# Attention, gated MLP and MoE on one core: the first three tiles' loads at once, the last routing, the sorting and the overflow list at other places

## The chip, the cores and the metric

The kernel runs on one core of a Trainium2 chip. The metric is the device time of one execution in microseconds. Three runs of the kernel before gave 929.73, 930.45 and 933.15 us; the median is 930.45.

## What is computed

Three layers follow each other over N = 3072 tokens (4 sequences of 768) of 384 numbers. All data are float32.

```python
# 1. attention with a decaying state: 8 heads of 48, per token t
cur = einsum('bhd,bhe->bhde', u * k[t], v[t])
y[t] = einsum('bhd,bhde->bhe', r[t], state + cur)
state = w[t][..., None] * state + einsum('bhd,bhe->bhde', k[t], v[t])
# 2. RMS norm and gated MLP, 384 -> 1536 -> 384
xn = x / sqrt(mean(x * x) + 1e-06) * rms_g
x = (silu(xn @ w_gate) * (xn @ w_val)) @ w_out
# 3. MoE: 8 experts, one per token, 384 -> 1024 -> 384
e_idx = argmax(x @ moe2_w_gate)
for e in range(8):
    mask = e_idx == e
    out[mask] = softmax_prob[mask, e] * sigmoid(x[mask] @ w_output_gate)[:, e] \
              * (relu(x[mask] @ w1[e]) @ w2[e])
```

The MLP's weights reach the kernel as 64-bit floating-point words, which it turns into float32 itself.

## The kernel before

**Numbers in two halves.** A matmul of float32 is made of three matmuls on a high and a low half (`mm3`, L163 to L167). The high half is written by ScalarE (ACT), the low half (value minus high half) by VectorE (DVE) or GpSimd (POOL), and TensorE (PE) needs both. For the experts' weights that is `split` (L133 to L135), for a relu `relu_split` (L870 to L878), for gathered tokens `transpose_in` (L572 to L583).

**The stretches.** Tokens go in tiles of 128 and the MLP in 8 blocks of 3 tiles. The attention of a tile is a Python generator, `attention` (L338 to L460), that issues a few instructions per step. The first three tiles and the first block of the MLP are the start; from then on each block's MLP runs with the attention of the next block and the routing of the block before between its matmuls, placed by a small table of slots (`Plan`). After the last block comes the second MoE, in units of tokens of one expert.

**The attention of a tile.** `load_tile` (L302 to L315) loads the features w, k and r in a transposed layout, as two pairs of DMAs on SyncE's (SP's) queue: w (96 KB each) and k with r (192 KB each). They land in one of two standing buffers, and tile 2's in a slot of the ring of weight buffers, which is free so early. Such a buffer has rows that no load writes; `pads` (L278 to L284) fills them, for tile 2 on POOL. `load_rk` (L317 to L321) loads r and k by rows (384 KB) into `rk`, of which there is one buffer; the generator of tile i asks for tile i+1's loads once its own data are used. `load_v` loads v (192 KB). Then follow the product r*k*u on POOL (L363, L364), its row sums g on DVE (L380), the output y (DVE, L384 and L424, and PE, L420), a copy of transposed k on ACT (L393) and the state's update.

**The MLP's weights.** 18 pieces are decoded (`decode`, L98 to L132), 12 of the first layer (a piece is one load of 384 KB from each of two matrices) and 6 of the second. A piece takes two DMAs, two passes on ACT (L113 and the high half), two on DVE (L114 and L118), one on POOL and one for the low half. The loads of pieces 0, 1 and 2 are issued ahead of everything (`advance(n, 1)`, L700 to L706); a `decode_step` then issues the loads of piece n+2 and decodes piece n.

**The hand-written start.** `START_SEQ` (L42, run by L711 to L719) is the order of the start: 0, 1 and 2 issue one step of that tile's attention, a negative number issues so many matmuls without use that keep TensorE awake, and 9 is a `decode_step`. All engines run their instructions in this order, so DVE takes up decode step 0 where the first 9 stands.

```python
advance(0, 1)
load_tile(1)
advance(1, 1)
load_v(1)
advance(2, 1)
load_tile(2)
load_v(2)
nc.gpsimd.memset(states, 0.0)
```

**The second MoE.** `route` (L519 and on) finds each token's expert, ranks the tokens within the experts with small matmuls (L552, L555) on the one-hot `oh` from DVE (L544), and scatters the rows to a place per expert in device memory (`scr`). The last block's routing runs inside unit 0 at slots `ROUTE_AT`; a unit has a slot after each group of first-layer matmuls (nine for one f) and of second-layer matmuls. When it is through, the gather of unit 1's tokens is issued on SP and `order()` (L905 to L931) adds up the counts on PE (L909), sorts the experts by size on DVE and hands their numbers to SP, which needs them for the addresses of all later weights and gathers. The units have fixed sizes (`FIRST`, `WINDOWS`: 256, 256, 272, 256, 432, ... tokens); units 0 and 1 are the first expert's, 2 and 3 the largest other one's, numbered from 0 here. Tokens beyond these sizes go on an overflow list, `tabd` in device memory, that `table()` (L933 to L979) makes on DVE in unit 2 at f = 2, and that is read at the end of the kernel. In each unit, f = 0 to 9: first-layer matmuls of f (while f < 8), relu, a share of the next expert's weights (load, split), second-layer matmuls of f - 2; at f = 6 the next unit's tokens are transposed and split.

## Time and profile before

| | |
|---|---|
| three runs | 929.73, 930.45, 933.15 us; median 930.45 |
| the profiled execution | 934.85 us, of which the span of instructions is 933.1 |
| mean granted clock of TensorE | 0.96 |
| PE, weight loads, DVE, ACT, POOL busy | 94%, 91%, 57%, 34%, 24% of the span |
| read and written in device memory | 73.22 MB and 16.73 MB, 96 GB/s over the span |

The profile is of one execution, taken by the hardware profiler. A busy share is an average over the whole span, in which the attention's start, the MLP and the MoE follow each other with limits of their own; so the slices of the span and windows of single stretches are read beside it. An engine's row in a timeline gives behind "[" how long the engine had idled before and, behind "<-", what ended that: `[12.63 <-DMA rk<-in_rkv_dram]` is an idle time of 12.63 us that ended when the load of `rk` landed. PE stands for matmuls, PEld for the weight loads ahead of them, which overlap. The granted clock is a share of TensorE's full rate of 2.4 GHz. "SPq" is SP's queue of DMA issues.

### The profile page before, as it was taken

How to read it: one execution, taken by the hardware profiler on the slowest of the kernel's cores; microseconds unless marked ns; L12 is line 12 of the kernel's file. 1: busy time of each engine (PE TensorE's matmuls, PEld its weight loads, DVE VectorE, ACT ScalarE, POOL GpSimd, SP SyncE). 2: the span in 40 equal slices, each digit the busy share in tenths (PEclk: the TensorE clock that was granted, in tenths of full speed). 3: DMA queues.
4: the chain of work that ended last, by engine and by line, in shares of the span. 5: the costliest groups of instructions: out<-in, count | busy, mean ns of one | idle time of the engine just before them, and what ended most of it. 6: DMA issues, size and time to landing. Idle time of an engine off the chain costs nothing. (4 is left out here: it accounts for less than half of the span.)

```text
span 933.1 us, 14620 instructions
## 1 busy us (share of the span) xinstructions
PE 876.9 (94%) x5543; PEld 846.7 (91%) x5543; DVE 533.7 (57%) x1073; ACT 314.8 (34%) x654; POOL 227.9 (24%) x298
## 2 busy tenths in 40 slices
PE   6568779999999999999999999999899999999995
PEld 4458769999999999999999999999899999999994
DVE  5589785656565376366456465434537565556551
ACT  1254433322322323323222322323334344434430
POOL 6465552212231131132123113010010100122111
PEclk7679899999999999999999999999999999999997
DMA  9564252274131023022122122001143453554510
GB/s 229 129 218 131 90 161 50 83 213 137 46 110 51 9 86 82 13 78 56 47 69 60 52 68 78 1 27 51 52 146 98 151 179 107 159 163 152 174 47 21
DMA packets 65300, 90.40 MB, mean 97 GB/s; under 512 B 6259, under 2 KB 56035, under 8 KB 65229
## 3 DMA queue, kind: packets, MB, share of 16 engines
q1 hardware_dynamic: 60973, 79.67, 29.2%
q0 software_dynamic: 3568, 9.57, 2.8%
q8 instruction: 44, 0.72, 0.3%
q10 hardware_dynamic: 688, 0.22, 0.1%
q14 instruction: 27, 0.22, 0.1%
HBM read 73.22 MB, written 16.73 MB: 96 GB/s over the span
## 5 line engine op out<-in xcount | busy, mean ns | idle before, releaser
L165 PE MATMUL a<-xh,gv 128*128 128x384 f32 x1152 | 324.1, 347 | 0.0
L165 PEld LDWEIGHTS a<-xh,gv 128*128 128x128 f32 x1152 | 213.7, 191 | 2.2
L165 PE MATMUL a<-xl,gv 128*128 128x384 f32 x576 | 195.9, 340 | 0.0
L500 DVE TENSOR_TENSOR sil<-a,sil 128x384 f32<-128x384 f32 x96 | 53.2, 554 | 110.6 <-PE a L165 110.2
L165 PE MATMUL a<-xh,w1s 128*128 128x256 f32 (+7 forms) x432 | 111.9, 325 | 1.4 <-DVE hl L876 1.1
L165 PEld LDWEIGHTS a<-xl,gv 128*128 128x128 f32 x576 | 110.3, 192 | 0.0
L502 ACT ACTIVATE hh<-sil 128x384 fp32r<-128x384 f32 x96 | 50.3, 524 | 162.2 <-DVE sil L500 162.2
L514 PE MATMUL l<-wo,hh 128*128 128x400 f32 x288 | 102.2, 355 | 0.0
L498 ACT ACTIVATE sil<-a 128x384 f32<-128x384 f32 x96 | 47.2, 492 | 156.7 <-PE a L165 151.6
L515 PE MATMUL l<-wo,hh 128*128 128x400 f32 x288 | 99.8, 347 | 0.0
L516 PE MATMUL l<-wo,hl 128*128 128x400 f32 x288 | 99.2, 345 | 0.0
L244 POOL DMA_INDIRECT out_dram<-row,iu x30 | 34.9, 1165 | 208.5 <-DVE row L887 188.7
L876 DVE SCALAR_TENSOR_TENSOR hl<-a,hh 128x256 fp32r<-128x256 f32 (+7 forms) x80 | 40.7, 510 | 74.3 <-ACT hh L875 74.3
L165 PEld LDWEIGHTS a<-xh,w1s 128*128 128x128 f32 x432 | 76.7, 188 | 2.8 <-DVE hl L876 1.6
L505 DVE TENSOR_TENSOR hl<-sil,hh 128x384 fp32r<-128x384 f32 x96 | 56.2, 585 | 34.9 <-ACT hh L502 34.9
L875 ACT ACTIVATE hh<-a 128x256 fp32r<-128x256 f32 (+7 forms) x80 | 36.5, 456 | 101.9 <-PE a L165 100.2
L165 PE MATMUL a<-xl,w1s 128*128 128x256 f32 (+7 forms) x216 | 69.7, 323 | 0.1
L384 POOL TENSOR_TENSOR y<-vt,g 128x384 f32<-128x384 f32 x23 | 22.0, 958 | 169.2 <-issue 62.6
L165 PE MATMUL l<-rows,hh 128*128 128x384 f32 (+3 forms) x240 | 63.0, 344 | 0.0
L420 PE MATMUL m<-vt,am 128*128 128x48 f32 x368 | 55.1, 278 | 4.5 <-DVE am L407 4.5
L420 PEld LDWEIGHTS m<-vt,am 128*128 128x128 f32 x368 | 51.2, 204 | 5.5 <-DVE am L407 5.4
L514 PEld LDWEIGHTS l<-wo,hh 128*128 128x128 f32 x288 | 54.9, 190 | 0.1
(216 smaller groups left out, 1510.8 us busy)
## 6 DMA issues: line engine op xcount, KB each, us to landing
raw<-in_moe_w_dram SPq DMA_DIRECT2D x64, 384.0 KB, 3.3
rk<-in_rkv_dram SPq DMA_DIRECT2D x24, 384.0 KB, 4.2
set<-in_feat_dram SPq DMA_DIRECT2D x46, 192.0 KB, 3.9
scr<-zrow SPq DMA_DIRECT2D x8, 788.0 KB, 7.6
set<-in_feat_dram SPq DMA_DIRECT2D x46, 96.0 KB, 3.0
vt<-in_rkv_dram SPq DMA_DIRECT2D x23, 192.0 KB, 2.5
raw<-in_moe_w_gate_dram SPq DMA_DIRECT2D x8, 384.0 KB, 4.0
raw<-in_moe_w_val_dram SPq DMA_DIRECT2D x8, 384.0 KB, 3.9
```

Source lines behind the costliest of these rows:

```text
L165: nc.tensor.matmul(o, a, b, start=start and i == 0, stop=stop and i == 2, skip_group_check=True)
L244: ins = nc.gpsimd.indirect_dma_start(out=dst, out_offset=bass.IndirectOffsetOnAxis(ap=idx, axis=0), in_=rows, in_offset=None, bounds_check ...
L420: nc.tensor.matmul(yp[:, 2 * p + q], am[q][:, p], vv[:, 2 * p + q], start=not ch, stop=True, skip_group_check=True,)
L498: nc.scalar.activation(out=sil, in_=o, func=AF.Silu)
L500: nc.vector.tensor_tensor(out=sil, in0=pg[1], in1=sil, op=ALU.mult)
L502: nc.scalar.activation(out=hh, in_=sil, func=AF.Copy)
L505: nc.vector.tensor_tensor(out=hl, in0=sil, in1=hh.bitcast(F32), op=ALU.subtract)
L514: nc.tensor.matmul(o, hh[:, sl], wh, start=f == 0, stop=False)
L515: nc.tensor.matmul(o, hh[:, sl], wl, start=False, stop=False)
L516: nc.tensor.matmul(o, hl[:, sl], wh, start=False, stop=f == KF - 1)
L875: nc.scalar.activation(out=hh, in_=o, func=AF.Relu)
L876: nc.vector.scalar_tensor_tensor(out=hl, in0=o, scalar=0.0, in1=hh.bitcast(F32), op0=ALU.max, op1=ALU.subtract)
```

## The change

- Tile 1's loads (features, r and k, v) are issued before the weights of piece 0, and tile 2's before those of piece 1. r and k of tiles 1 and 2 get two places in the ring of weight buffers (`more_rk`), and `load_rk` leaves out what is loaded already (`sets_rk`).
- The fills of tile 2's buffer, and the zeroing of the states, go from POOL to ACT (a copy scaled by 0 or 1); one strided fill stays on POOL.
- In `START_SEQ` the first 9 stands four places later.
- `ROUTE_AT` goes from (0, 1) to (0, 3); in unit 0 the gather of unit 1 stands at f = 2 and `order()` at f = 4.
- `table()` becomes a generator of five pieces, one each at f = 1 to 5 of unit 3, in place of one block at f = 2 of unit 2. Its DMA to `tabd` is issued on ACT's queue in place of SP's.

```diff
     out: bass.AP,
     FIRST=(256, 256),
     WINDOWS=((272, 256), (432,), (414,), (396,), (380,), (372,), (368,)),
-    ROUTE_AT=(0, 1),
+    ROUTE_AT=(0, 3),
     OFFS=((0, 0, 6.7, 7.5, 8.8, 10.5, 11.4, 11.5, 12.7), (0, 1.6, 3.2, 4.8, 6.4, 8, 9.6, 11.6, 13.8)),
     TGAP=(8.9, 9.0),
-    START_SEQ=(-11, 0, 0, 0, -4, -4, -6, -4, 0, 9, 1, 0, 1, -4, 0, 1, 1, 2, -4, 0, 0, 1, 9, 2, 0, 1, -4, 2, -6, 1, 9, 2, 1, 2, -4, 1, 2, 9, -2, 2, 2, 9, -6, 2, 9),
+    START_SEQ=(-11, 0, 0, 0, -4, -4, -6, -4, 0, 1, 0, 1, -4, 9, 0, 1, 1, 2, -4, 0, 0, 1, 9, 2, 0, 1, -4, 2, -6, 1, 9, 2, 1, 2, -4, 1, 2, 9, -2, 2, 2, 9, -6, 2, 9),
 ):
     nc = tc.nc
     B, S, _, H, D = rkv.shape
...
 
     def pads(t, engs):
 
-        for q in range(2):
-            engs[q].memset(t[64 * q + 32:64 * q + 64, KR:SETW], 1.0)
-        for q in range(2):
-            engs[q].memset(t[64 * q + 32:64 * q + 64, 0:KR], 0.0)
-        engs[1].memset(t[:, KR:SETW:SEG], 0.0)
+        for a, x in ((slice(KR, SETW), 1.0), (slice(0, KR), 0.0)):
+            for q in range(2):
+                rows = slice(64 * q + 32, 64 * q + 64)
+                if engs[q] is nc.scalar:
+                    nc.scalar.activation(
+                        out=t[rows, a], in_=one_b[rows, 0:1].to_broadcast([32, a.stop - a.start]),
+                        func=AF.Copy, scale=x,
+                    )
+                else:
+                    engs[q].memset(t[rows, a], x)
+        nc.gpsimd.memset(t[:, KR:SETW:SEG], 0.0)
 
     def parts(t):
 
...
     tiles = [(b, ch) for ch in range(NCH) for b in range(B)]
     vt = {}
     rk = {}
+    sets_rk = set()
     sets = {}
 
     def load_tile(i):
...
         b, ch = tiles[i]
         if i == NSET:
             t = ring_view([SETW], big=True)
-            pads(t, (nc.gpsimd, nc.gpsimd))
+            pads(t, (nc.scalar, nc.scalar))
         else:
             t = sets_w[(i - (i > NSET)) % NSET]
         sets[i] = t
...
             nc.sync.dma_start(out=kr[64 * q:64 * q + D], in_=feat[b, ch, q, :, 1:3])
 
     def load_rk(i):
-        if i < len(tiles):
+        if i < len(tiles) and i not in sets_rk:
             b, ch = tiles[i]
-            rk[i] = p1.tile([P, 2, H, D], F32, tag="rk", name="rk")
+            sets_rk.add(i)
+            if i in (1, 2):
+                rk[i] = more_rk[:, i - 1].rearrange("p (x h d) -> p x h d", x=2, h=H)
+            else:
+                rk[i] = p1.tile([P, 2, H, D], F32, tag="rk", name="rk")
             nc.sync.dma_start(out=rk[i], in_=rkv[b, ch * P:ch * P + P, 0:2])
 
     def load_v(i):
...
         load_rk(0)
         load_v(0)
         pads(sets_w[1], (nc.vector, nc.gpsimd))
+        load_tile(1)
+        more_rk = ring_view([2, 2 * DM], big=False)
+        load_rk(1)
+        load_v(1)
         kts = ring_view([NSET + 1, NPR * P], big=False).rearrange("p i (a t) -> p i a t", a=NPR)
         pieces = []
         for f in range(KF):
...
 
         turned = ring_view([4, KD * P], big=False)
         advance(0, 1)
-        load_tile(1)
+        load_tile(2)
+        load_rk(2)
+        load_v(2)
         advance(1, 1)
-        load_v(1)
         advance(2, 1)
-        load_tile(2)
-        load_v(2)
-        nc.gpsimd.memset(states, 0.0)
+        flat = states.rearrange("p b a d -> p (b a d)")
+        nc.scalar.activation(
+            out=flat, in_=one_b[:, 0:1].to_broadcast(flat.shape), func=AF.Copy, scale=0.0
+        )
 
         xs = new_x(0)
         first = [attention(c, a, xs[0], xs[1], a * P) for a in range(sizes[0])]
...
             return ids
 
         def table():
+
             left = q1.tile([P, E], F32, name="left")
             sh = [P, E, NOV]
             flag = q1.tile(sh, F32, name="flag")
...
             nc.vector.tensor_reduce(room, place, axis=AX.X, op=ALU.add)
             nc.vector.tensor_tensor(out=left, in0=cnt, in1=room, op=ALU.subtract)
             nc.vector.tensor_tensor(out=room, in0=room, in1=c["area"], op=ALU.add)
+            yield
             nc.vector.tensor_tensor(out=flag, in0=bc_e(left), in1=bc_k(c["thr"]), op=ALU.is_gt)
             flat = "p e k -> p (e k)"
             nc.vector.tensor_tensor_scan(
...
                 out=flag.rearrange(flat), in0=cum.rearrange(flat), scalar=c["pidx"],
                 in1=flag.rearrange(flat), op0=ALU.is_equal, op1=ALU.mult,
             )
+            yield
             nc.vector.tensor_tensor(out=tmp, in0=flag, in1=bc_e(c["eidx"]), op=ALU.mult)
             nc.vector.tensor_reduce(tab[:, 0:1], tmp.rearrange(flat), axis=AX.X, op=ALU.add)
+            yield
             nc.vector.tensor_tensor(out=tmp, in0=bc_e(room), in1=bc_k(c["thr"]), op=ALU.add)
             nc.vector.tensor_tensor(out=tmp, in0=tmp, in1=flag, op=ALU.mult)
             nc.vector.tensor_reduce(tab[:, 1:2], tmp.rearrange(flat), axis=AX.X, op=ALU.add)
+            yield
             nc.vector.tensor_tensor(out=cnt, in0=cnt, in1=c["area"], op=ALU.add)
             nc.vector.tensor_tensor(out=tmp, in0=flag, in1=bc_e(cnt), op=ALU.mult)
             nc.vector.tensor_reduce(tab[:, 2:3], tmp.rearrange(flat), axis=AX.X, op=ALU.add)
             nc.vector.tensor_copy(tabi, tab)
-            nc.sync.dma_start(out=tabd, in_=tabi)
+            nc.scalar.dma_start(out=tabd, in_=tabi)
+            yield
 
         def overflow(e, off):
 
...
         expert = [0]
         post = iter(())
         nxw = iter(())
+        listing = table()
         xg_cur, x_cur = xg0, (x0[:, 0], x0[:, 1])
         for ui, (k, r0, n) in enumerate(units):
             last_of = ui + 1 == NU or units[ui + 1][0] != k
...
                     if f >= 1:
                         next(post, None)
                 next(nxw, None)
-                if ui == 2 and f == 2:
-                    table()
+                if ui == 3 and f >= 1:
+                    next(listing, None)
                 if ui + 1 < NU:
                     if ui and f == 1:
                         xg_nxt = gather_unit(ui + 1)
...
                         else:
                             mm3(o, wh[:, cs], wl[:, cs], hh, hl, g == 0, g == KF2 - 1)
                     plan.step()
-                if ui == 0 and xg_nxt is None and not plan.at:
+                if ui == 0 and f == 2:
                     xg_nxt = gather_unit(1)
+                if ui == 0 and f == 4:
                     ids = order()
                     expert += [
                         nc.values_load(
```

**SP's queue at the start.** `set`, and `rv` from in_feat_dram, are the features of a tile (set_80: tiles 0 and 3, set_81: tiles 1 and 4, rv: tile 2), `raw` and `rv` from in_moe_w the words of a piece of MLP weights; both kernels begin with all of tile 0. After that and piece 0's two loads, before:

```order
L310 DMA set_81<-in_feat_dram 48x4x128 x2
L312 DMA set_81<-in_feat_dram 48x1024 x2
L109 DMA rv<-in_moe_w_gate_dram 128x3x256
L109 DMA rv<-in_moe_w_val_dram 128x3x256
L325 DMA vt<-in_rkv_dram 128x384
L109 DMA raw_141<-in_moe_w_out_dram 128x2x768
L310 DMA rv<-in_feat_dram 48x4x128 x2
L312 DMA rv<-in_feat_dram 48x1024 x2
L325 DMA rv<-in_rkv_dram 128x384
L310 DMA set_80<-in_feat_dram 48x4x128 x2
L312 DMA set_80<-in_feat_dram 48x1024 x2
L318 DMA rk<-in_rkv_dram 128x768
```

After tile 0 alone, now:

```order
L317 DMA set_81<-in_feat_dram 48x4x128 x2
L319 DMA set_81<-in_feat_dram 48x1024 x2
L329 DMA rv<-in_rkv_dram 128x768
L336 DMA vt<-in_rkv_dram 128x384
L109 DMA raw_138<-in_moe_w_gate_dram 128x3x256
L109 DMA raw_138<-in_moe_w_val_dram 128x3x256
L317 DMA rv<-in_feat_dram 48x4x128 x2
L319 DMA rv<-in_feat_dram 48x1024 x2
L329 DMA rv<-in_rkv_dram 128x768
L336 DMA rv<-in_rkv_dram 128x384
L109 DMA rv<-in_moe_w_gate_dram 128x3x256
L109 DMA rv<-in_moe_w_val_dram 128x3x256
```

The r and k of tile 1 (rk, the last row before) stand third now, ahead of the weights of piece 0; tile 2's four loads stand together ahead of piece 1's weights.

**PE in unit 0 of the second MoE.** The routing's first matmul (L524, now L535), the ranks from the one-hot (L552, now L563) and the counts of `order()` (L909, now L926) stand between the matmuls of the unit, first layer `a<-rv,w1s`, second layer `l<-rows`. Before:

```order
L165 MATMUL a<-rv,w1s 128x256 x9
L524 LDWEIGHTS one_b
L524 MATMUL m<-acc,one_b 128x8
L165 MATMUL a<-rv,w1s 128x256 x9
L552 LDWEIGHTS tri
L552 MATMUL m<-oh,tri 128x24
...
L909 LDWEIGHTS one_b
L909 MATMUL m<-acc,one_b 128x8
L165 MATMUL a<-rv,w1s 128x256 x9
L165 MATMUL l_6321<-rows_6055,hh_6333 128x384 x2
```

Now:

```order
L535 LDWEIGHTS one_b
L535 MATMUL m<-acc,one_b 128x8
L165 MATMUL a<-rv,w1s 128x256 x18
L165 MATMUL l_6320<-rows_6054,hh_6332 128x384 x2
L165 MATMUL l_6320<-rows_6054,hl_6333 128x384
L165 MATMUL l_6321<-rows_6054,hh_6332 128x384 x2
L165 MATMUL l_6321<-rows_6054,hl_6333 128x384
L563 LDWEIGHTS tri
L563 MATMUL m<-oh,tri 128x24
...
L926 LDWEIGHTS one_b
L926 MATMUL m<-acc,one_b 128x8
L165 MATMUL a<-rv,w1s 128x256 x9
```

Between the first routing matmul and the ranks stand 24 matmuls now, nine before; between the ranks and the counts stand 30 now and three small ones, before only these three.

**ACT in unit 3.** The relus of f = 5 to 7 (L875, now L892), the splits of weights (L134) and of the next unit's tokens (L580, now L591). Before:

```order
L875 ACTIVATE hh_7345<-a 128x256
L134 ACTIVATE rows_7351<-raw 128x768
L875 ACTIVATE hh_7370<-a 128x256
L134 ACTIVATE w1s<-raw 128x768
L580 ACTIVATE xh_7379<-m 128x432 x3
L875 ACTIVATE hh_7418<-a 128x256
```

Now:

```order
L892 ACTIVATE hh_7339<-a 128x256
L134 ACTIVATE rows_7345<-raw 128x768
L1002 DMA tabd<-tabi 128x4
L892 ACTIVATE hh_7369<-a 128x256
L134 ACTIVATE w1s<-raw 128x768
L591 ACTIVATE xh_7378<-m 128x432 x3
L892 ACTIVATE hh_7417<-a 128x256
```

The issue of the list's DMA stands between two relus; it waits for `tabi`, the last of the five pieces on DVE.

**DVE in unit 3.** Now, from f = 4 on, with a piece of the list (L994 to L996), the scales of the unit's tokens (L872 to L887, left out here), a relu's low half (L893), a weight split (L135) and the list's last piece:

```order
L135 TENSOR_TENSOR w1s<-raw,w1s 128x768
L994 TENSOR_TENSOR tmp<-rooms,thr 128x176
L995 TENSOR_TENSOR tmp<-tmp,flag 128x176
L996 TENSOR_REDUCE tab<-tmp 128x1
L872 TENSOR_REDUCE mx_7308<-xg 128x2
...
L893 SCALAR_TENSOR_TENSOR hl_7340<-a,hh_7339 128x256
L135 TENSOR_TENSOR rows_7345<-raw,rows_7345 128x768
L998 TENSOR_TENSOR cnt<-cnt,area 128x8
L999 TENSOR_TENSOR tmp<-flag,cnt 128x176
L1000 TENSOR_REDUCE tab<-tmp 128x1
L1001 CAST tabi<-tab 128x4
```

The pieces stand between the low halves that PE waits for; before, all of the list stood in one block between two low halves of unit 2.

## Rows read from the trace of the kernel before

**Rows 1.** Page, busy times and PE's slices: busy tenths of each 40th of the span

```profile
PE 876.9 (94%) x5543; PEld 846.7 (91%) x5543; DVE 533.7 (57%) x1073; ACT 314.8 (34%) x654; POOL 227.9 (24%) x298
...
PE   6568779999999999999999999999899999999995
```

**Rows 2.** Timeline, 0 to 75 us: start, us, engine, instruction, idle before, its releaser

```profile
9.76 0.60 ACT L393 ACTIVATE rv<-m 128x512 f32<-128x512 f32 x1 [6.21 <-PE m L391]
...
14.46 0.91 ACT L113 ACTIVATE raw<-raw 128x768 int32<-128x768 uint32 x1 [4.10 <-DMA raw<-in_moe_w_val_dram]
...
15.06 0.96 DVE L118 SCALAR_TENSOR_TENSOR dt<-raw,dt 128x768 uint32<-128x768 uint32 x1
...
21.72 0.56 DVE L424 TENSOR_TENSOR y<-m,y 128x384 f32<-128x384 f32 x1 [2.39 <-PE m L420]
...
24.33 0.35 SPq L318 DMA_DIRECT2D rk<-in_rkv_dram  x1
...
31.42 0.99 POOL L363 TENSOR_TENSOR rk<-rk 128x384 f32<-128x384 f32 x1 [12.63 <-DMA rk<-in_rkv_dram]
...
33.51 0.55 DVE L380 TENSOR_REDUCE g<-rk 128x8 f32<-128x384 f32 x1 [9.36 <-POOL rk L364]
...
37.06 0.55 DVE L114 TENSOR_SCALAR dt<-rv 128x768 uint32<-128x768 uint32 x1
...
62.67 0.33 PEld L165 LDWEIGHTS a<-xh,gv 128*128 128x128 f32 x1
```

**Rows 3.** Windows: start:end, length, busy PE PEld DVE ACT POOL, clock, DMA share, GB/s

```profile
5.00:30.00 25.00, 15.52 (x90) 11.19 (x89) 11.72 (x16) 2.61 (x5) 10.94 (x13) 0.71 1.06 252
20.00:25.00 5.00, 5.00 (x24) 4.42 (x23) 2.39 (x3) 1.10 (x3) 0.00 (x0) 0.50 1.01 188
```

**Rows 4.** DMA issues, 0 to 75 us: size of each, us from issue to landing

```profile
set<-in_feat_dram SPq DMA_DIRECT2D x8, 192.0 KB, 5.6
rk<-in_rkv_dram SPq DMA_DIRECT2D x4, 384.0 KB, 3.8
raw<-in_moe_w_gate_dram SPq DMA_DIRECT2D x4, 384.0 KB, 4.6
set<-in_feat_dram SPq DMA_DIRECT2D x8, 96.0 KB, 7.5
vt<-in_rkv_dram SPq DMA_DIRECT2D x4, 192.0 KB, 7.4
```

**Rows 5.** Timeline, unit 0 of the second MoE

```profile
673.14 0.19 PE L552 MATMUL m<-oh,tri 128*128 128x24 bf16 x1 [1.15 <-DVE oh L544]
...
675.15 0.19 PE L909 MATMUL m<-acc,one_b 128*128 128x8 bf16 x1 [1.75 <-DVE acc L569]
...
680.84 0.37 SPq L829 DMA_DIRECT2D xg<-scr  x1
...
692.81 0.82 PE L577 MATMUL m<-ident,xg 128*128 128x128 f32 x6
```

**Rows 6.** Windows, behind the two waits of unit 0

```profile
675.00:681.00 6.00, 5.85 (x25) 5.86 (x26) 2.13 (x10) 0.38 (x1) 3.15 (x6) 0.50 0.28 101
```

**Rows 7.** Timeline, unit 2

```profile
718.04 0.21 DVE L949 TENSOR_TENSOR place<-rank,eidx 128x64 f32<-128x64 f32 x1
...
723.76 0.39 PE L165 MATMUL a<-xh,w1s 128*128 128x272 f32 x1 [0.90 <-DVE hl L876]
```

**Rows 8.** Timeline, unit 3

```profile
737.72 0.42 DVE L876 SCALAR_TENSOR_TENSOR hl<-a,hh 128x256 fp32r<-128x256 f32 x1 [0.45 <-ACT hh L875]
...
743.79 0.96 DVE L135 TENSOR_TENSOR w1s<-raw,w1s 128x768 fp32r<-128x768 f32 x1 [0.72 <-ACT w1s L134]
...
746.84 0.84 ACT L134 ACTIVATE w1s<-raw 128x768 fp32r<-128x768 f32 x1
...
751.20 1.64 DVE L581 TENSOR_TENSOR xl<-m,xh 128x432 fp32r<-128x432 f32 x3 [1.87 <-ACT xh L580]
...
753.22 0.44 PE L165 MATMUL l<-rows,hl 128*128 128x384 f32 x1 [0.17 <-DVE hl L876]
```

## The prediction

> **What bounds the kernel now.** Read the busy times first: TensorE (PE) works 94% of the span [rows 1], so nearly all that can be saved is idle time of PE, or time in which it runs at half clock. Then look where PE idles. In the 40 slices [rows 1], 23.3 us each, that is the first six, 140 us, and one dent in the 29th, which ends near 677 us; the change touches the first 40 us, that dent and what follows it, and one wait at 723 us.
>
> *The start.* Read the timeline for who waits on what [rows 2]. VectorE (DVE) forms the row sums g of tile 1 at 33.51, after sitting idle for 9.36 us. It waited for GpSimd (POOL), whose product of r and k began at 31.42 after 12.63 us of idleness, and that waited for the r and k of tile 1, issued only at 24.33. The issue was late because one buffer held r and k (it was free only when tile 0 was through) and because the two loads of tile 3 stand ahead of it. From 5 to 30 us the 16 DMA engines are full, at 252 GB/s [rows 3]: what comes later in this queue arrives later. The first matmul of the gated MLP is at 62.67 [rows 2], and everything before it hangs on the tile chain through DVE.
>
> *The last routing.* In unit 0 of the second MoE, PE waits 1.15 us for the one-hot of DVE and 1.75 us for the new counts [rows 5]. Right after, 6 us run at a granted clock of 0.50 with PE busy 5.85 us [rows 6]; that is 1.2 GHz, so half of it, 2.9 us, is lost too.
>
> *The overflow list.* Its 18 DVE operations begin at 718.04 in one block, and PE waits 0.90 us, until 723.76, for the low half of a relu that stands behind them [rows 7].
>
> **The change part by part.**
>
> *Loads in the sequence of use.* The wait of 9.36 us goes: r and k of tiles 1 and 2 have buffers of their own and stand with their tiles in the queue. What is late next are the MLP weights, since tile 1 now stands ahead of the weights of decode step 0, and tile 2 ahead of those of step 1. Sizes [rows 4]: a tile is 2 x 96 + 2 x 192 + 384 + 192 = 1152 KB, a step's weights 2 x 384 = 768 KB. In the trace the weights of step 0 are there at 14.46, when ScalarE (ACT) starts on them [rows 2]. Now 1152 KB more come first (1.18 MB, 4.7 us at 252 GB/s): 19.1. The weights of step 1 come 1152 + 1152 + 768 = 3072 KB (3.15 MB, 12.5 us) after 14.46: 27.0. DVE is in order, and step 0 now stands ahead of the y of tile 0. Its passes take 0.55 and 0.96 [rows 2], so y may start at 20.6; it started at 21.72, so this wait costs nothing and may give up to 1.1. Step 1 began on DVE at 37.06; without the 9.36 that is 27.7, with the 1.1 it is 26.6, and its weights allow 27.0. The start therefore gains 9.4 to 10.1; I take **9.7**. At the slowest rate seen, 188 GB/s [rows 3], the weights of step 1 land at 31.2 and 5.9 is gained; with no wait at all it is 10.5.
> The DMA page of the Trainium skill (DMA: Bandwidth & Descriptors, section "Where 436 GB/s comes from") says that about 358 GB/s of HBM bind such a transfer. By that figure step 1's weights would land at an estimated 23.3 and the start would gain the 10.5. The row says 252, and the row is taken.
>
> *Fills moved to ACT.* Five fills (2 x 517, 2 x 1024 and 1536 columns, 4618 in all) go from POOL to ACT. A 512-column copy there takes 0.60 [rows 2], so they cost at most 5.4 us; ACT's first work besides a table load was that copy at 9.76, so they are hidden. If they overran, the copy, and with it the tile's state, would move one for one. Tile 2's loads wait for four of them, but stand tenth and later in a full queue. POOL gets to tile 0's product sooner, which is hidden behind DVE's wait for step 0. The other ring slot and the shifted first decode step add no instruction.
>
> *Last routing at slot 3, counts at f = 4.* Between the one-hot's start and its use PE now has one more block of nine matmuls and one of six, 15 matmuls, near 6 us at the 0.39 of [rows 7], against a wait of 1.15; between the new counts and their matmul it has four blocks. Both waits and the half clock behind them go: 1.15 + 1.75 + 2.9 = **5.8**. Bounds: 2.9 if the clock still falls, 5.8 if not; PE has no idle place left there, so the upper one. What moves behind: the expert numbers come later, so SyncE (SP) can issue the next weights only after them; the gather for unit 1 was issued at 680.84, on the last scatter's landing, and is needed where 692.81 now stands [rows 5], which moves to 687.0. That leaves 6.2 us, and loads take 3.8 to 7.5 [rows 4]: cost 0 to 1.3, I take 0.
>
> *The list in five pieces in unit 3, its write on ACT's queue.* The **0.9** at 723.76 goes. The 5.3 us of DVE work (718.04 to 723.3) move to steps 1 to 5 of unit 3. Between those steps DVE idles four times, from 0.45 to 0.72, 2.5 in all [rows 8], so the last piece ends 2.8 later than DVE would have been free. Of this the 1.87 before the next unit's split (751.20) swallow most; 1.0 reaches the relu of step 7, for which PE already waited at 753.22. Then the list's write: on ACT it must wait for the last piece, and behind it in order stand the relu of step 6 and a weight split of 0.84 [rows 8]. Issue (0.35, as on SP [rows 2]), relu and split then run late: 0 to 1.6 more, I take 1.1. Together **2.1 lost** (bounds 0 and 2.6).
> The same page (section "Issuing engines are not separate DMA queues") says that issuing a DMA from another engine saves only the issue time there. By that the move to ACT has nothing to give for its 1.1; with the write left on SP the loss would be 1.0. The row of 0.35 agrees.
>
> *Sum:* -9.7 - 5.8 - 0.9 + 2.1 = **-14.3 us**. The profiled execution takes 934.85 (span 933.1); it becomes 920.6. It is 4.4 above the median of the three runs, 930.45, which becomes **916.2**.
>
> **The rivals.**
>
> 1. *Slow loads.* The queue runs at 188 GB/s as from 20 to 25 us, the start gains 5.9: 920.0. For it: 6 us at that rate are in the trace; against: the same stretch averages 252.
> 2. *The clock falls in unit 3.* PE idles about 2 us there, and a stretch like [rows 6] follows: 2.9 more, 919.1. For it: 1.15 and 1.75 did it in unit 0. Against: the two waits I reckon with here, 1.0 and 1.1, are both shorter than either of those.
> 3. *Nothing is lost in unit 3*, because relus run before they are needed: 914.1.
> 4. *The gather is late at the end of unit 0:* 1.3 lost, 917.5.
> 5. *Block 0 eats the start's gain:* its PE waits for decoded weights; if those were bound by their loads and not by DVE, 9.7 come back, 925.9, no change that can be measured. Against: the sixteen steps left load 16 x 786 KB = 12.6 MB, 50 us at 252 GB/s, and PE's weak slices last to 140 us.
> 6. *Slower:* DVE, in order, waits for MLP weights ahead of tile work. The place is decode step 1, the price one for one: once its weights land after 37.06 the start loses, and once they land after 41.7 (37.06 + 5.8 + 0.9 - 2.1) the kernel does. That needs 3.15 MB in 27 us, 116 GB/s; at 100 it would be 46.0 and 934.8. Against: the slowest 5 us of the full queue had 188.
>
> **How the numbers follow.** Chances: forecast 0.55, slow loads 0.12, clock 0.12, no loss 0.10, late gather 0.05, block 0 eats it 0.04, slower 0.02. A measurement of this kernel can tell about 0.5% (4.7 us) from no change. All but the last two lie under 925.8: faster 0.94, same 0.04, slower 0.02. The range takes in rivals 1 to 4, the first two together (922.9), the bounds of the start (down to 913.3 with no loss in unit 3) and the runs' own scatter of 1 to 2 us: 911.5 to 924.
>
> **What would show it.** Right: DVE's g of tile 1 follows its rq without idling, before 25 us; decode step 1 begins near 27.4; the MLP's first matmul is near 53; no PE wait and no 0.50 clock in unit 0; PE waits near the end of unit 3 for a low half, some 2 us. Wrong: PE waits for the first gather; ACT's first kt copy is late; the first matmul comes later than 57, or the time from it to unit 0 grows.

## The result: 12 us less, and the profile after

The changed kernel takes **918.97 us** (median; 918.80 to 919.52) against 931.03 before (929.73 to 933.15; one more run of it than was known at the prediction): ratio **0.987**, 95% interval 0.9858 to 0.9883, a gain of 12.1 us with some 1.1 to either side. The forecast was 916.2 in a range of 911.5 to 924.0, with a gain of 14.3. So the sign, the range and the places are right, and the gain was put 2.2 us too high (1.3 by a second timing, below). The terms didn't err alike, and one sentence on a variant that was not built was wrong by several us; the runs below show both.

The page after, busy times and PE's slices, answers to [rows 1]:

```profile
PE 880.5 (96%) x5543; PEld 849.0 (93%) x5543; DVE 534.2 (58%) x1073; ACT 319.6 (35%) x659; POOL 225.1 (25%) x293
...
PE   7987889999999999999999999999999999999994
```

The work is the same (5543 matmuls, 1073 operations of DVE), and the dent in the 29th slice is gone.

**Where the time went.** The start of the first matmul of each stretch, from the timelines, gives the length of each. The kernel before stands there twice, with the profile of the forecast and with a second one (the first experiment below):

| stretch, us | before, first profile | before, second | after | after less second |
|---|---|---|---|---|
| start, to the MLP's first matmul | 62.73 | 59.40 | 51.62 | -7.8 |
| block 0 of the MLP | 109.26 | 110.87 | 109.95 | -0.9 |
| blocks 1 to 7 | 497.57 | 497.57 | 497.57 | 0 |
| second MoE, unit 0 | 24.36 | 23.23 | 18.84 | -4.4 |
| unit 1 | 19.21 | 19.22 | 19.21 | 0 |
| unit 2 | 20.45 | 20.44 | 19.26 | -1.2 |
| unit 3 | 20.45 | 20.45 | 22.04 | +1.6 |
| unit 4 to the end | 179.08 | 179.01 | 178.96 | 0 |
| span | 933.1 | 930.2 | 917.5 | -12.7 |

Against the second profile the stretches give the timed 12.1 within its interval; against the first they would give 15.6, which the timed runs don't show.

**The start after.** Timeline of the changed kernel, answers to [rows 2] (start, us, engine, instruction, idle before and its releaser):

```profile
17.20 0.56 DVE L114 TENSOR_SCALAR dt<-raw 128x768 uint32<-128x768 uint32 x1 [1.24 <-DMA raw<-in_moe_w_val_dram]
...
18.67 0.55 DVE L435 TENSOR_TENSOR y<-m,y 128x384 f32<-128x384 f32 x1
...
18.89 1.83 POOL L122 TENSOR_TENSOR dt<-dt,raw 128x768 int32<-128x768 int32 x1 [2.08 <-DVE dt L118]
...
19.14 2.67 DVE L384 TENSOR_TENSOR_SCAN rq<-set,front 128x516 f32<-128x516 f32 x1
...
22.46 0.54 DVE L391 TENSOR_REDUCE g<-rv 128x8 f32<-128x384 f32 x1
...
24.09 0.90 ACT L113 ACTIVATE rv<-rv 128x768 int32<-128x768 uint32 x1 [0.47 <-DMA rv<-in_moe_w_val_dram]
...
25.99 1.23 DVE L114 TENSOR_SCALAR dt<-rv 128x768 uint32<-128x768 uint32 x1
...
31.09 1.22 DVE L384 TENSOR_TENSOR_SCAN rq<-rv,front 128x516 f32<-128x516 f32 x1
...
51.62 0.67 PE L165 MATMUL a<-xh,gv 128*128 128x384 f32 x1
```

The row sums g of tile 1 follow without an idle time, at 22.46; the wait of 9.36 us is gone. What DVE waits for now is piece 0's weights, 1.24 us at 17.20. Decode step 1 begins at 25.99, 1.9 us after its weights: they don't bind. From there to the MLP's first matmul it is 25.6 us, as before (37.06 to 62.73). From 20 to 25 us DVE is the busiest engine now, 4.92 of 5 us, with POOL at 4.72 (windows, columns as in [rows 3]):

```profile
20.00:25.00 5.00, 4.10 (x27) 3.58 (x26) 4.92 (x7) 1.88 (x4) 4.72 (x5) 0.50 1.06 370
```

**Unit 0 after.** Timeline, answers to [rows 5]:

```profile
663.54 0.19 PE L563 MATMUL m<-oh,tri 128*128 128x24 bf16 x1
...
668.00 0.18 PE L926 MATMUL m<-acc,one_b 128*128 128x8 bf16 x1
...
670.74 0.37 SPq L846 DMA_DIRECT2D xg<-scr  x1
...
676.87 0.82 PE L588 MATMUL m<-ident,xg 128*128 128x128 f32 x6
```

The window of the same stretch, answers to [rows 6]:

```profile
663.00:669.00 6.00, 6.00 (x47) 5.67 (x47) 3.45 (x17) 1.50 (x5) 3.13 (x6) 1.00 0.19 67
```

Both waits are gone, the clock stays at its full level of 2.4 GHz, and PE is busy all of the 6 us, with 47 matmuls where 25 ran at half of it. The gather is issued 6.1 us ahead of its use (6.2 was reckoned), and PE doesn't wait for it.

**Unit 3 after.** Timeline, answers to [rows 8]. "ACTq" is the issue of a DMA on ACT:

```profile
732.99 0.17 DVE L1001 CAST tabi<-tab 128x4 int32<-128x4 f32 x1
...
733.19 0.35 ACTq L1002 DMA_DIRECT2D tabd<-tabi  x1
...
733.64 0.38 ACT L892 ACTIVATE hh<-a 128x256 fp32r<-128x256 f32 x1 [3.26 <-PE a L165]
...
735.67 1.63 DVE L592 TENSOR_TENSOR xl<-m,xh 128x432 fp32r<-128x432 f32 x3
...
736.35 0.62 PE L165 MATMUL l<-rows,hh 128*128 128x384 f32 x2 [0.76 <-ACT hh L892]
...
737.22 0.41 DVE L893 SCALAR_TENSOR_TENSOR hl<-a,hh 128x256 fp32r<-128x256 f32 x1
...
737.68 0.44 PE L165 MATMUL l<-rows,hl 128*128 128x384 f32 x1 [0.72 <-DVE hl L893]
```

ACT is idle for 3.26 us until the list's last piece (tabi) is there and its write is issued, with the relu of f = 6 behind it. (The row names PE's matmuls as the releaser; the relu starts when the issue, 733.19 and 0.35 long, is over.) PE then waits twice at the end of the unit, 0.76 for a high and 0.72 for a low half: 1.5 of the 1.6 us.

### The profile page after: what moved, and what is told of

The parts are those of the page before. It is cut to its first block, busy times and chain, and to the rows that moved or that the text cites. A ratio compares the mean times of both kernels' runs of the same rounds, so it can differ in the third digit from the quotient of the medians.

```text
span 917.5 us, 14623 instructions
## 1 busy us (share of the span) xinstructions
PE 880.5 (96%) x5543; PEld 849.0 (93%) x5543; DVE 534.2 (58%) x1073; ACT 319.6 (35%) x659; POOL 225.1 (25%) x293
## 5 line engine op out<-in xcount | busy, mean ns | idle before, releaser
L893 DVE SCALAR_TENSOR_TENSOR hl<-a,hh 128x256 fp32r<-128x256 f32 (+7 forms) x80 | 40.6, 509 | 72.4 <-ACT hh L892 68.3
L516 DVE TENSOR_TENSOR hl<-sil,hh 128x384 fp32r<-128x384 f32 x96 | 58.1, 605 | 34.9 <-ACT hh L513 34.9
L892 ACT ACTIVATE hh<-a 128x256 fp32r<-128x256 f32 (+7 forms) x80 | 36.5, 456 | 100.1 <-PE a L165 96.2
L527 PEld LDWEIGHTS l<-wo,hl 128*128 128x128 f32 x288 | 55.2, 192 | 0.2
```

Source lines behind the costliest of these rows:

```text
L516: nc.vector.tensor_tensor(out=hl, in0=sil, in1=hh.bitcast(F32), op=ALU.subtract)
L527: nc.tensor.matmul(o, hl[:, sl], wh, start=False, stop=f == KF - 1)
L892: nc.scalar.activation(out=hh, in_=o, func=AF.Relu)
L893: nc.vector.scalar_tensor_tensor(out=hl, in0=o, scalar=0.0, in1=hh.bitcast(F32), op0=ALU.max, op1=ALU.subtract)
```

## The experiments

All were timed beside the kernel before, in three groups, each on one chip. The kernel before had a median of 931.68, 931.60 and 932.11 there.

| kernel | median | ratio (95%) |
|---|---|---|
| before again | 931.31 | 0.9994 (0.9982 to 1.0006) |
| start alone | 922.59 | 0.9895 (0.9880 to 0.9911) |
| routing alone | 926.56 | 0.9943 (0.9926 to 0.9959) |
| list alone | 932.21 | 1.0002 (0.9992 to 1.0012) |
| the change again | 918.59 | 0.9862 (0.9843 to 0.9882) |
| list's write on SP | 921.77 | 0.9877 (0.9854 to 0.9899) |
| list in unit 4, write on SP | 917.63 | 0.9840 (0.9823 to 0.9856) |
| first decode step at its old place | 923.44 | 0.9908 (0.9892 to 0.9923) |
| one buffer for r and k | 929.14 | 0.9974 (0.9964 to 0.9984) |
| fills on POOL | 919.63 | 0.9871 (0.9856 to 0.9886) |
| sorting right behind the routing | 921.17 | 0.9890 (0.9874 to 0.9905) |
| list in unit 4, one step ahead of decode | 917.58 | 0.9845 (0.9832 to 0.9859) |

### The kernel before, once more

No edit.

> The kernel before, unchanged, profiled again. Theory A (the first profile was a slow draw: it took 934.85 where the four timed runs have a median of 931.03): the new profiled execution lies between 929.5 and 932, and one stretch of it is shorter by 2 to 5 us than in the first profile, the start up to the second MLP block (172.0 us) or unit 0 of the second MoE (24.4 us). Theory B (the offset belongs to what the profile shows): it lies at 934 to 935 again, and the gain of 15.6 us between the two spans is the true one, so that the timed difference of 12.1 would come out larger here. Ratio 1.000 within 0.002 by both.

Measured: the profiled execution took 931.92 us, its span 930.2, ratio 0.9994. Its start, in the timeline:

```profile
11.83 0.90 ACT L113 ACTIVATE raw<-raw 128x768 int32<-128x768 uint32 x1 [1.85 <-DMA raw<-in_moe_w_val_dram]
...
21.05 0.35 SPq L318 DMA_DIRECT2D rk<-in_rkv_dram  x1
21.12 0.56 DVE L424 TENSOR_TENSOR y<-m,y 128x384 f32<-128x384 f32 x1 [2.39 <-PE m L420]
...
30.18 0.55 DVE L380 TENSOR_REDUCE g<-rk 128x8 f32<-128x384 f32 x1 [6.63 <-POOL rk L364]
...
33.72 0.55 DVE L114 TENSOR_SCALAR dt<-rv 128x768 uint32<-128x768 uint32 x1
...
59.40 0.67 PE L165 MATMUL a<-xh,gv 128*128 128x384 f32 x1
```

and the window behind the two waits of unit 0:

```profile
673.40:679.40 6.00, 5.97 (x32) 5.97 (x33) 2.47 (x10) 0.77 (x2) 3.16 (x6) 0.72 0.28 101
```

Theory A holds in the main: the first profile was a slow draw. In the first profile the weights of piece 0 were there 2.6 us later (14.46 against 11.83), the load of r and k was issued 3.3 us later (24.33) and DVE waited 9.36 in place of 6.63; the MLP's first matmul came 3.3 us later. Up to the second MLP block only 1.7 us of that are left (172.0 against 170.3, where theory A said 2 to 5), since block 0 took 1.6 us longer here. Why the first draw was slow stays open. The routing-only and the list-only kernel have the same start as the kernel before, and with 59.15 and 59.22 us both stand with the second profile. The half clock in unit 0 lasted shorter here, too: 0.72 over the 6 us in place of 0.50, and the unit took 1.1 us less. In the profiles of the start-only and the list-only kernel, which have the same two waits, the unit takes 24.35 and 24.31, as in the first profile.

### The three parts of the change, each alone

Start: the hunks on START_SEQ, `pads`, `load_rk`, `load_tile` and the order of the loads. Routing: these lines:

```diff
-    ROUTE_AT=(0, 1),
+    ROUTE_AT=(0, 3),
...
-                if ui == 0 and xg_nxt is None and not plan.at:
+                if ui == 0 and f == 2:
                     xg_nxt = gather_unit(1)
+                if ui == 0 and f == 4:
```

List: `table()` as a generator, `listing`, and the write on ACT.

> Only the loads, fills and the later first decode step; routing, sorting and list as before. By the sum of the prediction 9.7 us less; by the two traces the first matmul of the MLP at 51.6 us in place of 62.7 (11.1 less) and the second block 10.4 earlier: the median falls by 10.4, ratio 0.989. Rival (the waits of block 0 for decoded weights take more of it in other executions): 6 to 8 less, ratio 0.992 to 0.9935. Unit 0 stays 24.4 us long, units 2 and 3 20.45 each.

> Only the last routing at slot 3, the gather at f = 2 and the sorting at f = 4. Unit 0 at 18.9 us in place of 24.4 in the profile. If half the clock follows the two waits in every execution, the median falls by 5.5, ratio 0.994; if in some executions only (theory A), by 2.9 to 4.5, ratio 0.995 to 0.997.

> Only the overflow list in five pieces in unit 3 with its write on ACT's queue. By the two traces unit 2 is 1.2 us shorter and unit 3 1.6 longer: 0.4 us slower, ratio 1.0004. By the prediction 0.9 less and 2.1 more: 1.2 slower, ratio 1.0013. Rival (nothing lost in unit 3): 0.9 to 1.2 faster, ratio 0.999.

Measured: 9.1 us less, 5.1 less, 0.5 more (not to be told from nothing). The sum is 13.7; the whole change gave 12.1 and 13.0 in its two timings. In the traces the MLP's first matmul of the start-only kernel is at 51.15; unit 0 of the routing-only kernel takes 18.86 and all of it runs at full clock; units 2 and 3 of the list-only kernel take 19.26 and 22.52, with the same two waits at the end, in its timeline:

```profile
749.22 0.62 PE L165 MATMUL l<-rows,hh 128*128 128x384 f32 x2 [0.84 <-ACT hh L875]
...
750.55 0.44 PE L165 MATMUL l<-rows,hl 128*128 128x384 f32 x1 [0.71 <-DVE hl L876]
```

The two waits make 1.55 of the 2.1 us by which unit 3 is longer. So nothing shows that the parts touch each other, and the list's part by itself brings nothing: it moves its loss from unit 2 to unit 3.

### The change, once more

No edit.

> The changed kernel, unchanged, again, as the reference of the three variants beside it and for the scatter of its profile: 919 us within 0.6, its MLP's first matmul between 51.0 and 52.0 us, unit 0 of the second MoE 18.8 us and unit 3 22.0 us long, as in its first profile. If its start scatters like that of the kernel before (59.2 to 62.7 over four profiles), the first matmul may lie up to 3 us elsewhere.

Measured: 918.59 (918.24 to 920.50); the MLP's first matmul at 51.51, unit 0 18.85, unit 3 22.09. Over the six profiles that have the new start whole (two of the change, and those of the start alone, of the write on SP, of the list in unit 4 and of the sorting behind the routing) the first matmul lies between 50.53 and 51.62; three of the four with the old start lie between 59.15 and 59.40, the fourth at 62.73. Whether the new start scatters less, so few profiles can't tell.

### The list's write on SP

```diff
-            nc.scalar.dma_start(out=tabd, in_=tabi)
+            nc.sync.dma_start(out=tabd, in_=tabi)
```

> The list's write is issued on SP again, the five pieces stay in unit 3. Theory (the write holds ACT until the last piece, and with it the relu of f = 6, by which the two last waits of the unit come): unit 3 at 20.5 to 20.9 us in place of 22.0, the time 1.1 to 1.5 less, near 917.7. By the prediction's term, 1.1 less. Rival (the pieces on DVE alone delay the low halves): unit 3 stays at 21.5 or more, the time within 0.5 of the changed kernel's.

Measured: 3.2 us **slower** than the change beside it (five of the six executions at 920.9 to 922.05, above all four of the change, and one at 916.3, which no trace explains and by which the two intervals overlap). Unit 3 did what theory says: 20.65 us. The loss is in unit 4, 36.16 us in place of 30.4, where neither theory looked. The waits of SP's queue, 715 to 750 us (engine and line, what it waited for, us in total, times, longest):

```profile
SPq L1002 <- DVE hl L893: 7.2, 1, 7.2
```

and the timeline, from the last load ahead of the write to PE's wait:

```profile
724.14 0.37 SPq L139 DMA_DIRECT2D raw<-in_moe_w_dram  x1
...
731.18 0.17 DVE L1001 CAST tabi<-tab 128x4 int32<-128x4 f32 x1
...
731.37 0.37 SPq L1002 DMA_DIRECT2D tabd<-tabi  x1
...
731.98 0.38 SPq L152 DMA_DIRECT2D raw<-in_moe_w_dram  x1
...
737.35 0.85 ACT L134 ACTIVATE w1s<-raw 128x768 fp32r<-128x768 f32 x1 [3.28 <-DMA raw<-in_moe_w_dram]
...
738.23 0.96 DVE L135 TENSOR_TENSOR w1s<-raw,w1s 128x768 fp32r<-128x768 f32 x1 [2.96 <-ACT w1s L134]
...
741.86 0.73 PE L165 MATMUL a<-xh,w1s 128*128 128x432 f32 x1 [2.87 <-DVE hl L893]
```

and the window of what follows:

```profile
740.90:747.70 6.80, 5.84 (x16) 5.40 (x17) 2.93 (x5) 1.44 (x3) 2.17 (x5) 0.50 0.51 173
```

For 7.2 us SP's queue stands at the write, until the last piece is there. (The view names the low half hl as what ended the wait; the write is issued right after `tabi`, 731.18 and 0.17 long.) The first load behind it is issued 17.4 us into unit 3, in the changed kernel 11.3 us. ACT and DVE split these weights of the next expert late and stand still meanwhile, with the relu of unit 4 in line behind the splits; PE waits 2.87 us, and from 740.9 to 747.7 the granted clock is 0.50, 1.2 GHz. On ACT's queue the same write holds one relu and the split behind it.

The Trainium skill (DMA: Bandwidth & Descriptors, section "Issuing engines are not separate DMA queues") says that issuing from another engine saves only the time it takes to issue. The trace differs for a write that has to wait: the issue is 0.37 us long, and what the other queue saves SP is the 7.2 us for which the write holds back the issues behind it.

### The list in unit 4, its write on SP

```diff
-                if ui == 3 and f >= 1:
+                if ui == 4 and f >= 1:
...
-            nc.scalar.dma_start(out=tabd, in_=tabi)
+            nc.sync.dma_start(out=tabd, in_=tabi)
```

> The write on SP and the five pieces in unit 4, of 432 tokens, where DVE idles 1.2 to 1.9 us at each f. Theory: unit 3 back at 20.45, unit 4 unchanged at 30.4: 1.6 less than the changed kernel, 917.4. Rival (a list piece is late for something in unit 4 too): unit 4 over 30.8 and no gain against the kernel with the write on SP alone.

Measured: 917.63, 1.0 less than the change beside it. Unit 3 takes 20.46 and unit 4 30.37. Windows of the two units, 718.4 to 738.8 and 738.9 to 769.2:

```profile
718.40:738.80 20.40, 20.22 (x143) 19.19 (x142) 13.20 (x31) 10.61 (x23) 4.04 (x7) 1.00 0.49 160
738.90:769.20 30.30, 30.30 (x157) 28.32 (x156) 21.79 (x50) 13.31 (x25) 2.18 (x5) 1.00 0.43 140
```

The 18 operations of the list (50 on DVE in unit 4 now, 32 without) cost nothing there: PE is busy for all of its 30.3 us. The gain in the trace is the 1.6 us of theory; the medians' 1.0 has it within their scatter. In this profile block 0 took 112.6 us, with one stretch of 17 us at half clock; that scatter, not the edit, makes this execution the slowest of its five (919.53).

### The first decode step at its old place

```diff
-... -4, 0, 1, 0, 1, -4, 9, 0, 1, 1, 2, ...
+... -4, 0, 9, 1, 0, 1, -4, 0, 1, 1, 2, ...
```

> The first decode step stands at its old place in the start, all else as changed. Theory (DVE is in order: it then waits for the weights of piece 0, which land near 17, ahead of tile 0's decay products and tile 1's first scan, 3.6 us of work): the MLP's first matmul 2.4 to 3.6 us later, 921.4 to 922.6. Rival (the early loads alone make the gain, DVE has slack): within 0.5 of the changed kernel.

Measured: 923.44, 4.9 more than the change beside it; the MLP's first matmul at 56.37, 4.9 later. Theory holds in kind and was low in size. DVE in the timeline:

```profile
16.42 0.56 DVE L114 TENSOR_SCALAR dt<-raw 128x768 uint32<-128x768 uint32 x1 [4.17 <-DMA raw<-in_moe_w_val_dram]
...
23.68 0.56 DVE L435 TENSOR_TENSOR y<-m,y 128x384 f32<-128x384 f32 x1 [2.39 <-PE m L431]
```

DVE waits 4.17 us for the weights. The decay products that it makes after that are late for PE, and so DVE waits again, 2.39 us, for PE's sums: in all 6.6 of waits, where the change has 1.24. That the late products are the cause of the second wait is read from the order of the rows, not tested. The two 4.9 are of different executions: the profiled one is the fastest of the five (920.77), and its block 0 took only 106.7 us, at a mean granted clock of 0.93 (109.1 at 0.90 in the change beside it); the other four lie between 923.2 and 923.6.

### One buffer for r and k

```diff
-            if i in (1, 2):
-                rk[i] = more_rk[:, i - 1].rearrange("p (x h d) -> p x h d", x=2, h=H)
-            else:
-                rk[i] = p1.tile([P, 2, H, D], F32, tag="rk", name="rk")
+            rk[i] = p1.tile([P, 2, H, D], F32, tag="rk", name="rk")
...
-        load_rk(1)
...
-        load_rk(2)
```

> The early loads in the new order, but r and k in their one old buffer: tile 1's r and k are asked for only when tile 0 is through with it, behind all the early loads in SP's queue. Theory (the buffer is the greater part of the start's gain): the issue near 18 us, the product on POOL near 26 to 28, DVE's row sums of tile 1 at 27 to 29 in place of 22.5, the MLP's first matmul 4.5 to 6.5 us later than in the changed kernel, 923 to 925. Rival (the order of the loads makes the gain alone): within 1 us of the changed kernel's 918.8.

Measured: 929.14, 10.2 more than the change. Theory holds, and more than it said: without the buffer all of the start's gain is gone. The timeline, SP, POOL and DVE:

```profile
19.39 0.35 SPq L324 DMA_DIRECT2D rk<-in_rkv_dram  x1
...
28.19 0.99 POOL L369 TENSOR_TENSOR rk<-rk 128x384 f32<-128x384 f32 x1 [13.82 <-DMA rk<-in_rkv_dram]
...
30.28 0.55 DVE L386 TENSOR_REDUCE g<-rk 128x8 f32<-128x384 f32 x1 [9.55 <-POOL rk L370]
```

The load is issued a little earlier than before, at 19.39, and stands behind even more loads: 8.8 us until POOL has it. The MLP's first matmul is at 60.81. The new order without the buffer is worth nothing. The buffer with the old order was not built, so what it would be worth by itself is not shown.

### The fills on POOL

```diff
-            pads(t, (nc.scalar, nc.scalar))
+            pads(t, (nc.gpsimd, nc.gpsimd))
...
-        nc.scalar.activation(
-            out=flat, in_=one_b[:, 0:1].to_broadcast(flat.shape), func=AF.Copy, scale=0.0
-        )
+        nc.gpsimd.memset(states, 0.0)
```

> The five fills on POOL again, all else as changed. By the prediction they are hidden on either engine: DVE waits 1.2 us for the weights of decode step 0 behind them, so 0 to 0.8 us more, 918.6 to 919.6. Rival (POOL reaches tile 0's product 3 us or more later, beyond that slack, and tile 2's loads wait for the fills): 2 us or more, 921 or above.

Measured: 919.63, 0.7 to 1.0 more than the change's two medians, and the intervals overlap: nothing that this measurement tells. POOL's product begins at 10.78 in place of 8.97, g of tile 0 at 12.89 in place of 12.14, and the MLP's first matmul is at 51.27, no later. The fills are hidden, as the prediction said.

### The sorting right behind the routing

```diff
-                if ui == 0 and f == 2:
+                if ui == 0 and xg_nxt is None and not plan.at:
                     xg_nxt = gather_unit(1)
-                if ui == 0 and f == 4:
```

> The routing at slot 3, but the sorting again right behind it at f = 2, so that PE waits for the new counts (1.75 us before) and no longer for the one-hot. If the half clock follows this one wait: unit 0 about 4.7 to 5.2 us longer than the changed kernel's 18.85, 923.3 to 924. If one wait does not bring it: 1.75 longer, 920.4.

Measured: 921.17 (919.52 to 922.47); unit 0 takes 20.01 us, 1.2 more than with the change. PE's one wait there, in the timeline:

```profile
664.06 0.18 PE L926 MATMUL m<-acc,one_b 128*128 128x8 bf16 x1 [1.37 <-DVE acc L580]
```

and the window of the whole unit:

```profile
658.10:678.00 19.90, 18.29 (x133) 17.71 (x131) 9.84 (x46) 6.04 (x15) 3.65 (x7) 1.00 0.25 81
```

One wait of 1.37 us costs 1.2 and the clock stays at its full level. The half clock of the kernel before came with two waits, 1.15 and 1.75, and is gone when one of them is. The median is 2.2 above the change's, more than the trace's 1.2; four executions that lie 3 us apart don't settle that.

### The list in unit 4, and a step of tile 1 ahead of the first decode step

The edit of the list in unit 4, and:

```diff
-... -4, 0, 1, 0, 1, -4, 9, 0, 1, 1, 2, ...
+... -4, 0, 1, 0, 1, -4, 1, 9, 0, 1, 2, ...
```

> The list in unit 4 with its write on SP, and in the start one step of tile 1 (its second scan, product and row sums) ahead of the first decode step: DVE works on them while it waits for piece 0's weights, and the scan is out of the way of POOL's 1.8 us addition, beside which it took 2.67 us in place of 1.23. Theory: the scan at 16 us in 1.23 us, the second scan pair 1 us earlier, the MLP's first matmul 0.5 to 1.3 earlier, and 1.0 to 1.6 from the list: 916.0 to 917.2. Rival (another two-input operation of DVE meets POOL's addition, and the gain is lost): 917.6, as with the list alone.

Measured: 917.58, ratio 0.9845. The rival holds: the gain is the list's alone, and the MLP's first matmul is at 51.76. DVE and POOL in the timeline:

```profile
15.47 2.02 DVE L384 TENSOR_TENSOR_SCAN rq<-set,front 128x516 f32<-128x516 f32 x1
...
20.78 1.83 POOL L122 TENSOR_TENSOR dt<-dt,raw 128x768 int32<-128x768 int32 x1 [0.95 <-DVE dt L118]
21.04 2.67 DVE L368 TENSOR_TENSOR_SCAN kq<-rv,back 128x516 f32<-128x516 f32 x1
```

The scan that was moved is out of the addition's way, and the next scan, of tile 2, stands in it now and takes 2.67 us. The moved scan isn't free either: it takes 2.02 us in place of 1.23, since a product of POOL that began at 15.07 runs beside it until 16.40.

## Why the prediction was right, and where it was off

**The direction and the places** were right: all that moved is in the start, in unit 0, in unit 2 and in unit 3, and blocks 1 to 7 and the rest are the same to 0.1 us. The wait of DVE for r and k, both waits of unit 0 with the half clock behind them, and the wait of unit 2 went, and unit 3 got a new one.

**Start, -9.7 forecast: 7.8 by one pair of profiles, 9.1 timed alone (8.3 to 11.2 by its interval).** The mechanism is the one that was forecast; the size was taken from a draw, since the wait of 9.36 is from an execution whose start was 3.3 us longer than in three other profiles of the same code. Against that execution the start fell by 11.1, more than the 10.5 reckoned for no wait at all. By the second profile the same working gives: wait 6.63 gone; y of tile 0 2.45 earlier (21.12 to 18.67, where I allowed 1.1); 1.44 back, since a scan of DVE took 2.67 in place of 1.23. Sum 7.6; step 1 moved from 33.72 to 25.99, by 7.7. The last item has no place in the prediction at all. Over all profiles, the MLP's first matmul lies at 60.1 us on average in the four with the old start and at 51.1 in the six with the new one, 9.0 earlier. So the term was too large by 0.6 to 2.1 us, and the timing, whose interval holds 9.7, does not tell it from right.

**The weights' landing.** I took 252 GB/s and had the weights of step 1 at 27.0; they were there at 24.09. The rate was right and the base was off again: piece 0's weights landed at 14.46 in the first profile and at 11.83 in the second. From there 12.5 us more give 24.3. So the weights never bound, and the 25 us of the queue ran at 263 GB/s, near the 252 of [rows 3]. The estimate of 23.3 by the Trainium skill's 358 GB/s (DMA: Bandwidth & Descriptors, section "Where 436 GB/s comes from") came close only because it stood on the late landing; from 11.83 the same figure gives an estimate of 20.6.

**From the profile to the median.** I took the first profile's 4.4 us above the median as an offset that stays: 920.6 for the profile after, 916.2 for the median. It was a draw. The profile after took 919.14, the median 918.97. That step, *"It is 4.4 above the median of the three runs"*, is the weak one: of the 4.4, 3.3 stood in the start, so a gain that was worked out from the slow start was taken off a median that doesn't have it. With 7.6 for the start, as above, the prediction's own sum is -7.6 - 5.8 - 0.9 + 2.1 = -12.2, and 930.45 - 12.2 is 918.3; with the 9.1 that was timed it is 916.8. That the draw makes all of the 2.2 us is therefore likely and not shown.

**Unit 0, -5.8 forecast: 5.5 against the first profile, 4.4 against the second; 5.1 timed alone.** Right. The two waits, 1.15 and 1.75, are in all four profiles with the old routing; what scatters is the half clock behind them, 6.8 us in three of the four (the unit 24.3 to 24.4 long) and 3.4 in the fourth (23.2).

**Unit 2, -0.9 forecast: -1.2.** Right; the 0.3 beyond the one wait is in no single row.

**Unit 3, +2.1 forecast: +1.6.** Right in place and kind. The write waits for the last piece on ACT's queue, and the relu of f = 6 and the split behind it run late. With the write on SP unit 3 lost 0.2 in place of 1.6, so that nearly all of the loss is ACT's; of the 1.0 that I gave to the pieces alone little is left.

**The write left on SP: "the loss would be 1.0".** Wrong, and by a rule that the prediction itself had used for DVE: what is queued behind the waiting instruction. I looked at ACT's queue and not at SP's, where the loads of unit 4 stand. The loss was 3.2 us more than with the write on ACT.

**The rivals.** Slow loads, no (263 GB/s). Nothing lost in unit 3, no (1.6). Half clock in unit 3, no: its two waits of 0.76 and 0.72 leave it at 1.00. A late gather, no. Block 0 gave nothing back that can be told from its scatter (109.1 and 109.9 us in the changed kernel, 109.3 and 110.9 before, 106.7 to 112.6 over all profiles). DVE's wait for MLP weights is there, 1.24 us for step 0, and at its old place in the sequence it was 4.17: moving the first decode step is worth 4.9 us of the change, and the prediction gave it no price of its own. Slower, no.

## What to carry to other kernels

Before a sum is made from one profile, see how its execution lies among the timed runs; if it lies at their edge, the stretch that makes it long is a draw, and terms from that stretch are too large. A DMA that waits for a late result holds all that is queued behind it: put it on the queue whose next work is least urgent, or issue it where the result is already there. An order of loads is worth nothing where a buffer isn't free for them: here the new order without the second places in the buffer gained nothing.

The fastest versions were those with the list in unit 4, 917.6 us, 1.0 below the change where they ran side by side; the trace gives 1.6 for it, the interval of the medians can't tell it from 0.

## What the runs showed of the hardware

**DVE and POOL stand in each other's way.** The scan rq (L384) of 516 columns takes 1.22 or 1.23 us in 22 of 24 tiles of the changed kernel, and 2.67 and 2.90 in the two in which POOL's addition of 768 columns runs (19.14 and 106.44 us); where a 1-column operation of POOL begins after it, it takes 1.22 (31.09). The step that moves the scan brought 2.67 us to another one. At 19.14 the addition had begun 0.25 us ahead of the scan, and it was the scan that took longer; at 8.69 the scan began first, and POOL's product beside it took 1.73 us, where the same product takes 0.99 at 14.42. Timeline of the changed kernel:

```profile
8.69 1.23 DVE L384 TENSOR_TENSOR_SCAN rq<-set,front 128x516 f32<-128x516 f32 x1
...
8.97 1.73 POOL L374 TENSOR_TENSOR rk<-rk 128x384 f32<-128x384 f32 x1 [2.71 <-DMA vt<-in_rkv_dram]
...
14.42 0.99 POOL L374 TENSOR_TENSOR rv<-rv 128x384 f32<-128x384 f32 x1
```

The Trainium skill (SBUF — State Buffer, section "SBUF: two separate sides") says that the two engines share a pair of ports, that the operation that starts first holds it to its end, and that the other one is blocked; for DVE this holds of operations with two inputs from SBUF, as the scan has, against one of GpSimd that reads SBUF. The trace agrees: 1.58 us of the scan's 2.67 lie beside the addition, and 1.44 is what it lost; at 106.44 it is 1.80 and 1.68.

**TensorE's clock.** It stayed at 2.4 GHz through one wait of 1.37 us and through two of 0.76 and 0.72; it fell to 1.2 GHz with two of 1.15 and 1.75, for 6.8 us (674.4 to 681.2 us in the first profile of the kernel before; 3.4 in the second), and with one of 2.87, for 6.8 (740.9 to 747.7, the write on SP). So a wait can cost twice its length (unit 4 was 5.8 us longer for 2.87 of wait), and the price differs between executions of one kernel.
